# A dense and a dilated attention mixed by a gate, on one core: head pairs in the outer loop instead of query chunks

## The chip, the cores and the metric

The kernel runs on one core of one Trainium2 chip. The time is the device time of one launch in microseconds (us). Of three runs of the kernel before, the median was 818.75 us (816.8 to 819.12). A core has five engines with an instruction queue each: TensorE (PE, matrix products and transposes), VectorE (DVE), ScalarE (ACT), GpSimd (POOL) and SyncE (SP, which issues the transfers here). An engine runs its own instructions in their order and waits on semaphores for the others.

## The reference

Two attentions over the same input, 2048 positions of 512 values, 32 heads of 16. Branch A is dense: every query attends to all 2048 keys. Branch B attends to eight keys at distances 0, 2, ..., 14. A gate per position mixes them.

```python
x = A_x                                     # 1 x 2048 x 512, bf16
g = sigmoid((x * gate_w).sum(-1, keepdims=True))
# A: q, k, v = x @ A_wqkv in 32 heads of 16
scores = einsum("bhqd,bhkd->bhqk", q, k) * 16 ** -0.5
a = softmax(scores) @ v                     # then heads joined, @ A_wo
# B: q, k, v = x @ B_wqkv; idx = pos - (0, 2, ..., 14), masked below 0
logits = einsum("bhsd,bhswd->bhsw", q, k[idx]) * 16 ** -0.5
b = softmax(logits) @ v[idx]                # then heads joined, @ B_wo
return g * a + (1 - g) * b
```

The 32 x 2048 x 2048 exponentials of branch A are the bulk of the work.

## The kernel before

*A planner writes the order.* The program is not written down in loops. Every piece of work is an `Op` (line 73) with an engine, a planned duration, what it depends on, a due time, and the buffers (`Hold`, `Slots`) that it takes and gives back. `Sched.run` (line 253) plays a model of the engines: again and again it takes the engine whose next piece can start soonest, picks among its ready pieces the one due first, and emits it. Each engine's instructions then stand in that order for good: the chip cannot reorder them, it only waits. An `Op` may also have a `not_before` time.

*Branch A* is cut into 32 periods (line 1028): a query chunk `c_` of 512 positions (4 of them, `NC`) and a head group `i` of four heads (8 of them, `NG`). In the old order the chunk is the outer loop and the head group the inner one. In a period, PE makes scores of 128 keys by 512 queries per head (16 key tiles x 4 heads = 64 such units) into PSUM. Most units go to ACT: rings of alternately three and two units (`emit_fill`), one exponential instruction each (tile `pT`). A part goes to DVE instead (`start_quad`, `make_quad`): four units make a quad. DVE computes an exponential by converting to integers that are read as bf16 bit patterns: four conversions (`dt<-m_ps`) and two further terms (`dt<-dt`, shifted). `d_source` starts a quad when DVE has room. PE multiplies all with the values into one accumulator `acc` (`emit_pva`, `emit_pvd`). When a period is through, `post` (line 916) transposes the accumulator on DVE, takes the reciprocal, scales on POOL (`ott`), and, after the second head group of a pair, transposes back into `oat` (128 x 512, bf16): 16 of these, one for each chunk and pair.

*Projections.* Keys of all groups stay in SBUF, in `kt_all` (128 x 8 groups x 2048, bf16), values in `vp_all`. `k_proj` (line 537) makes keys of one group and chunk: 20 matmuls on PE, a cast and a maximum on DVE; `selk` joins the maxima. `v_proj` (line 588) makes values of some heads. `q_proj` (line 633) makes the queries of one period; three buffers. `g_jobs` (line 674) computes the gate. When which is issued is set in `hooks` (line 1393), which is called as a period begins, with due times in units of `TPER` = 23,500 planned ns. In the old order period 0 asks for the keys of all groups, spread over some six periods, and values come in periods 0, 2 and 4; the weights `wo` (`wo_jobs`, line 492) are loaded in period 7 into the place of the weights of keys and values.

*Branch B* comes in 16 tiles of 128 positions (`b_tile`, line 706), beside A. For each, PE projects, DVE copies, SP stores keys and values to a scratch tensor in DRAM, loads them back shifted (`ksh`, `vsh`, eight shifts), and POOL multiplies and adds (`prod`), with small steps on DVE (`smmax`, `smsum`) and ACT (`smexp`) between. POOL's last step makes `obb`; PE transposes it (`fin2`) and DVE copies it to `obt` (128 x 4 x 128). `hooks` starts tile t when 1.7 t <= p + 1.

*Finals.* `final` (line 967) makes 128 rows of the output: PE multiplies `obt` with B's output weights, DVE scales by 1 - g (`fb`), PE multiplies the chunk's four `oat` with `wo`, DVE scales by g and adds (`osb`), SP stores. In the old order it is asked for after each chunk's last head group (`after_post`, line 1430). For the last chunk it is done in two parts: three pairs first, their sums kept in the place of the keys of the first groups (`fa_view`, line 960), and the last pair at the end. `oat` has six buffers and `obt` five.

*Zero passes.* PE's planner adds products with zeros (`zero_pass`, line 1373) where it would otherwise do too little.

Of the kernel before, what the change touches and what calls it, by code (L numbers as in the profile page):

```python
# [20 lines left out]
NG = 8  # L21
W = 8
DIL = 2
QW = 512
# [307 lines left out]
def kernel(  # L332
# [19 lines left out]
    TPC = QW // 128  # L352
    BPC = QW // 32
    WH = W // 2

    const = ctx.enter_context(tc.tile_pool(name="const", bufs=1))
    work = ctx.enter_context(tc.tile_pool(name="work", bufs=2))
# [42 lines left out]

    COL4 = [("c", j, 512) for j in range(4)]
    S_ = Sched()
    for name_, n_ in (("m", 2), ("rA", 1), ("rB", 1), ("acc", 1), ("pTA", 3), ("pTB", 3), ("qt", 3), 
                      ("dt", 8), ("accT", 2), ("ott", 2), ("ksv", 2), ("prod", 1), ("lg", 2),
                      ("kvs", 1), ("qb", 1), ("osb", 3), ("oat", 6), ("obt", 5), ("fb", 1)):
        S_.slots[name_] = Slots(n_)

    def misc_ps(hold, shape, dtype=FP32):
        return ps.tile(shape, dtype, tag=f"m{hold.k}", bufs=1, name=f"m{hold.k}_ps")
# [127 lines left out]
    def k_proj(i, sc, due, first=False):  # L537
        hold = Hold("m")
        st = {}

        def part(c0, c1):
            def s():
                if c0 == 0:
                    st["pk"] = misc_ps(hold, [128, QW])
                    mm_init(st["pk"], e32, QW)
                pk = st["pk"]
                for c in range(c0, c1):
                    for j in range(4):
# [12 lines left out]
        def red():  # L561
            src = st["pk"][:] if first else kt_all[:, i, sc * QW:(sc + 1) * QW]
            V.tensor_reduce(out=kmax_all[:, i, sc:sc + 1], in_=src, axis=AX.X, op=ALU.max, apply_absolute_value=True)
        p1 = Op("PE", part(0, 2), mms=COL4 * 3, deps=xt_ops[sc] + [ld["wk"]], due=due, acq=[hold], name="k1")
        p2 = Op("PE", part(2, DC), mms=COL4 * 2, deps=[p1], due=due, name="k2")
        for o in (p1, p2):
            S_.add(o)
        if first:
            r = S_.add(Op("DVE", red, dur=700.0, deps=[p2], due=due, name="kred"))
            e = S_.add(Op("ACT", evac, dur=650.0, deps=[p2, r], due=due, rel=[hold], name="kev"))  # L570
        else:
            e = S_.add(Op("DVE", evac, dur=690.0, deps=[p2], allow=400.0, rel=[hold], name="kev"))
# [15 lines left out]
    def v_proj(h0, h1, tb, TB, due):  # L588
# [17 lines left out]
            V.tensor_copy(out=vp_all[:, tb:tb + TB, h0:h1, 0:DH], in_=st["pv"][:].rearrange("p t (h d) -> p t h d", d=DH))  # L606
        per = max(1, TB // 2) * DC
        deps = [o for sc in range(tb // TPC, (tb + TB - 1) // TPC + 1) for o in xt_ops[sc]] + [ld["wv"]]
        ops = [Op("PE", mk(0), mms=[("f", None, max(n, 140))] * per, due=due, acq=[hold], name="v1")]
        if TB > 1:  # L610
            ops.append(Op("PE", mk(1), mms=[("f", None, max(n, 140))] * per, due=due, name="v2"))
        ops.append(Op("DVE", evac, dur=690.0, allow=400.0, rel=[hold], name="vev"))
# [85 lines left out]
        g_done.append(ops[-1])  # L698


    kv_store = {}
    obt_tiles, obt_hold, obt_ops = {}, {}, {}
    ob_last = {}
# [2 lines left out]
    def b_tile(t, due):  # L706
# [19 lines left out]
        def store():  # L726
            SP.dma_start(out=kv_scr[16 + t * 128:16 + (t + 1) * 128, :], in_=st["kvs"][:])
        xd = xt_ops[t // TPC] + [ld["bw"]]
        kv = [Op("PE", pj("k", hk, 0, 2), mms=COL4 * 2, deps=xd, due=due, acq=[hk, hkv], name="bk1"),
              Op("PE", pj("k", hk, 2, 4), mms=COL4 * 2, due=due, name="bk2"),  # L730
              Op("DVE", kev, dur=690.0, allow=600.0, rel=[hk], name="bkev")]
        vv = [Op("PE", pj("v", hv, 0, 2), mms=COL4 * 2, deps=xd + [kv[1]], due=due, acq=[hv], name="bv1"),
# [154 lines left out]
                level[-1] += 1  # L887
        padd(fin1, 1264.0, acq=[hobb], rel=[hp[2]])
        hb = Hold("m")
        obt_hold[t] = Hold("obt")  # L890

        def fin2():
            st["ptp"] = misc_ps(hb, [128, DC, 128], BF16)
# [4 lines left out]
                                identity=ident[:], tile_position=(0, 32 * c4))  # L898

        def fin3():  # L900
            obt_tiles[t] = sb(obt_hold[t], [128, DC, 128], BF16, "obt")
            V.tensor_copy(out=obt_tiles[t][:], in_=st["ptp"][:])
        f = [Op("PE", fin2, mms=[("c", j, 128) for _ in range(DC) for j in range(4)], allow=4000.0, acq=[hb, obt_hold[t]], rel=[hobb],
                deps=[pool[-1]], name="bf2"),
             Op("DVE", fin3, dur=420.0, allow=800.0, rel=[hb], name="bf3")]
# [10 lines left out]
    def post(c_, i, pv_ops):  # L916
        acc = acc_tiles[(c_, i)]
        pair, half = (c_, i // 2), i % 2
        hT = Hold("accT")
        st = {}  # L920
        if not half:
            oat_hold[pair] = Hold("oat")
            ott_of[pair] = (Hold("ott"), {})
        ho, so = ott_of[pair]
        last = (c_, i) == (NC - 1, NG - 1)

        def turn():
            accT = sb(hT, [128, BPC, 32], FP32, "accT")
            V.transpose(out=accT[:].rearrange("p b d -> p (b d)"), in_=acc[:])
            st["accT"] = accT  # L930

        def rec():
            rden = work.tile([128, BPC], FP32, name="rden", tag="rden", bufs=3)
            V.reciprocal(out=rden[:], in_=st["accT"][:, :, DH:DH + 1].rearrange("p b o -> p (b o)"))
            st["rden"] = rden

        def scale():
            if not half:
                so["ott"] = sb(ho, [128, BPC, 32], BF16, "ott")
            rd_bc = _ap(st["rden"][:], [list(st["rden"][:].ap[0]), [1, BPC], [0, DH]])  # L940
            (V if last else G).tensor_tensor(out=so["ott"][:, :, half * DH:half * DH + DH], in0=st["accT"][:, :, 0:DH], in1=rd_bc,
                                             op=ALU.mult)

        def back():
            oat_tiles[pair] = sb(oat_hold[pair], [128, QW], BF16, "oat")
            V.transpose(out=oat_tiles[pair][:], in_=so["ott"][:].rearrange("p b d -> p (b d)"))
        a = 0.0 if last else 3000.0
        ops = [Op("DVE", turn, dur=720.0, allow=-2000.0, deps=pv_ops, acq=[hT],
                  rel=[acc_hold[(c_, i)]], name="accT", prompt=True),
               Op("DVE", rec, dur=240.0, allow=a, name="rec"),  # L950
               Op("DVE" if last else "POOL", scale, dur=450.0 if last else 640.0, due=-1.0, acq=[] if half else [ho], rel=[hT],
                  name="scale")]
        if half:
            ops.append(Op("DVE", back, dur=710.0, allow=a, acq=[oat_hold[pair]], rel=[ho], name="oatT"))
        S_.chain(ops)
        if half:
            oat_ops.setdefault(c_, []).append(ops[-1])


    def fa_view(tt):  # L960
        flat = kt_all[:, 0:NG - 1, :].rearrange("p g s -> p (g s)")
        return flat[:, tt * 2 * QW:(tt + 1) * 2 * QW].bitcast(FP32)

    fa_ops = {}
    NPR = NG // 2

    def final(c_, tt, k0, k1, due):

# [56 lines left out]
            fa_ops[tt] = ops[-1]  # L1025


    periods = [(c_, i) for c_ in range(NC) for i in range(NG)]
    NP = len(periods)
    front = [0] * NP  # L1030
    back = [NT] * NP
# [361 lines left out]
    def hooks(p):  # L1393
        now = S_.now
        c_, i = periods[p]
        if p == 0:
            g_jobs(now + 12000.0)
            for g in range(1, NG):
                reds = [k_proj(g, sc, now + TPER * (0.85 * (g - 1) + 0.1 * (sc + 1))) for sc in range(NC)]
                selk(g, reds, now + TPER * (0.85 * (g - 1) + 0.45))  # L1400
        if p == 0:
            q_proj(periods[1][0], periods[1][1], now + 0.4 * TPER)
        if p + 2 < NP:
            q_proj(periods[p + 2][0], periods[p + 2][1], now + 0.6 * TPER)
        if p == 0:
            v_due(4, 8, now, TPER * 0.9)
            v_due(8, 16, now + TPER * 0.3, TPER * 1.5)
        if p == 2:
            v_due(16, 24, now, TPER * 1.8)
        if p == 4:  # L1410
            v_due(24, 32, now, TPER * 1.8)
        if p == NG - 1:
            wo_jobs([o for i_ in range(NG) for o in kt_ops[i_]] + list(vp_ops.values()))
        if p < 31:
            for t in range(NT):
                if 2 * t == p or (p == 0 and t == 0) or (t in (1,) and p == 1):
                    pass
        while b_next[0] < NT and b_next[0] * 1.7 <= p + 1.0:
            b_tile(b_next[0], now + (2000.0 if p > 2 else 12000.0))
            b_next[0] += 1  # L1420

    b_next = [0]

    def v_due(h0, h1, t0, span):
        n = (h1 - h0) * DH
# [3 lines left out]

    def after_post(c_, i):  # L1430
        now = S_.now
        if c_ < NC - 1 and i == NG - 1:
            for tt in range(TPC):
                final(c_, tt, 0, NPR, now + TPER * (0.5 + 0.6 * tt))
        if c_ == NC - 1 and i == NG - 2:
            for tt in range(TPC):
                final(c_, tt, 0, NPR - 1, now + TPER * 0.15 * (tt + 1))
        if c_ == NC - 1 and i == NG - 1:
            for tt in range(TPC):
                final(c_, tt, NPR - 1, NPR, now)  # L1440
# [42 lines left out]
```

## Time and profile before

| | |
|---|---|
| median of three runs | 818.75 us |
| the profiled execution: its time | 817.6 us |
| its span, first to last instruction | 815.5 us |
| mean granted clock of PE | 0.986 |
| busy: PE, DVE, ACT, POOL | 746.9, 677.0, 761.2, 695.1 us |
| first exponential starts | 26.9 us |
| last exponential ends | 802.9 us |
| POOL's first product starts, last ends | 53.8, 804.8 us |

All durations below come from the profiled execution. A row of the groups reads: line, engine, operation, what it writes and reads with the shapes, the count, busy time and mean duration in ns, then the engine's idle time just before these instructions and what ended it. Line 381 is a helper that records each operation, so the groups are told apart by their tiles. A row of the stages reads: from:to, length, busy us and (in brackets) instructions of PE, PE's weight loads, DVE, ACT and POOL, the granted clock, the share of DMA, GB/s. The order of the instructions in both programs can be read from the built programs, without a run; where the text says that something stands "at exponential 32", 32 of ACT's 656 exponential instructions were emitted before it.

### The profile page before, as it was taken

Reading aid. Unit: us, or ns where it says so; the run is one execution under the profiler, and the core shown is the slowest. Engines: PE = TensorE matmul, PEld = TensorE weight load, DVE = VectorE, ACT = ScalarE, POOL = GpSimd, SP = SyncE. Lnnn points to the kernel's source line nnn. Section 1 sums busy time; section 2 is a strip of 40 time slices with the busy share of each in tenths; the row PEclk is TensorE's granted clock in tenths of the full one; section 3 lists DMA queues with packets and bytes.
Section 4 is the critical chain, followed back from the end, with each engine's and each line's share of the span. In section 5 each row is a group of like instructions: output and inputs, shape, how many; then the busy total and the mean of one; then the engine's idle time right before and its main releaser. Section 6 shows DMA issues by size and latency. Waiting matters only on the chain.

```text
span 815.5 us, 20495 instructions
## 1 busy us (share of the span) xinstructions
PE 746.9 (92%) x8593; PEld 242.5 (30%) x8647; DVE 677.0 (83%) x1023; ACT 761.2 (93%) x682; POOL 695.1 (85%) x599
## 2 busy tenths in 40 slices
PE   8899999999989999999999898889998998999896
PEld 3334333333223232222222222222222232222222
DVE  2456677988799887999999897897999889999984
ACT  2798999899799998999999999999999999999993
POOL 1037694986799899999999999999999999999994
PEclk9999999999799999999999999998999999999998
DMA  8020304003211112112122212111211221101100
GB/s 269 18 67 14 105 2 118 2 14 117 79 52 66 47 41 83 41 54 66 52 66 67 65 31 92 37 40 53 66 66 53 59 79 60 52 10 46 52 2 27
DMA packets 44155, 47.47 MB, mean 58 GB/s; under 512 B 2080, under 2 KB 41504, under 8 KB 44064
## 3 DMA queue, kind: packets, MB, share of 16 engines
q1 hardware_dynamic: 44064, 46.18, 17.6%
q8 instruction: 67, 1.10, 0.6%
q14 instruction: 24, 0.20, 0.1%
HBM read 39.85 MB, written 6.32 MB: 57 GB/s over the span
## 4 chain that ended last, share of the span: by engine, by line
ACT 32%; POOL 26%; PE 22%; issue 10%; DVE 9%; POOLq 0%; ACTq 0%; DVEq 0%
ACT pT L381 31%; POOL prod L381 23%; PE m_ps L381 10%; DVE dt L381 7%; PE acc L381 6%; PE ring L381 5%; POOL lg L381 2%; PE warm L381 1%; POOL obb L381 1%; POOL ott L381 1%; PE pxt L381 1%; ACT lg L381 0%; DVE accT L381 0%; DVE osb L381 0%; POOL vp_all L381 0%
## 5 line engine op out<-in xcount | busy, mean ns | idle before, releaser
L381 ACT ACTIVATE pT<-ring 128x1536 bf16<-128x1536 f32 (+1 forms) x656 | 750.7, 1292 | 21.5 <-PE ring L381 19.6
L381 PE MATMUL ring<-qt,kt_all 32*128 32x512 bf16 x1640 | 278.8, 385 | 34.9 <-ACT pT L381 30.2
L381 POOL TENSOR_TENSOR prod<-prod 128x512 f32<-128x512 f32 x224 | 294.0, 1318 | 10.4
L381 DVE TENSOR_SCALAR dt<-m_ps 128x512 uint16<-128x512 f32 x408 | 268.5, 676 | 35.3 <-PE m_ps L381 23.1
L381 POOL TENSOR_TENSOR prod<-ksh,qb 128x512 f32<-128x512 bf16 x128 | 162.7, 1298 | 70.3 <-DMA ksh<-kv_scr 68.2
L381 DVE TENSOR_SCALAR dt<-dt 128x2048 uint16<-128x2048 uint16 x204 | 221.6, 1090 | 0.5 <-PE acc L381 0.3
L381 PEld LDWEIGHTS <-kt_all 32*128 32x128 bf16 x2048 | 86.5, 91 | 281.5 <-issue 274.3
L381 PE MATMUL acc<-pT,vp_all 128*17 128x512 bf16 x1640 | 158.3, 386 | 2.9 <-issue 2.8
L381 POOL TENSOR_TENSOR prod<-vsh,lg 128x512 f32<-128x512 bf16 x128 | 151.7, 1202 | 4.5
L381 PE MATMUL m_ps<-qt,kt_all 32*128 32x512 bf16 x408 | 140.8, 384 | 10.0 <-DVE dt L381 5.8
L381 PEld LDWEIGHTS <-vp_all 128*17 128x17 bf16 x2048 | 46.4, 88 | 107.0 <-issue 97.8
L381 PE MATMUL acc<-dt,vd_all 128*17 128x512 bf16 x816 | 63.2, 385 | 0.1
L381 PE MATMUL m_ps<-bw,xT 128*32 128x512 bf16 x768 | 54.5, 382 | 0.7 <-DVE dt L381 0.7
L381 PE MATMUL acc<-ones_t,zw 128*32 128x512 bf16 (+1 forms) x225 | 47.9, 392 | 2.6 <-issue 1.3
L381 PE MATMUL acc<-dt,vp_all 128*17 128x512 bf16 x408 | 40.7, 389 | 1.0 <-issue 1.0
L381 PEld LDWEIGHTS <-xT 128*32 128x32 bf16 (+1 forms) x1152 | 31.9, 96 | 31.2 <-issue 24.1
L381 PEld LDWEIGHTS <-zw 128*32 128x32 bf16 (+1 forms) x419 | 21.8, 95 | 57.3 <-issue 54.2
L381 PE MATMUL m_ps<-xT,wq 128*16 128x512 bf16 x512 | 38.7, 387 | 0.0
L381 DVE CAST kt_all<-m_ps 128x512 bf16<-128x512 f32 x28 | 19.1, 684 | 22.0 <-PE m_ps L381 21.9
L381 PE MATMUL m_ps<-xT,wkv 128*16 128x512 bf16 x512 | 36.7, 380 | 0.0
L381 DVE CAST qt<-m_ps 128x512 bf16<-128x512 f32 x32 | 21.8, 682 | 10.5 <-PE m_ps L381 10.2
L381 DVE TENSOR_SCALAR absq<-m_ps 128x512 int32<-128x512 int32 x32 | 21.9, 684 | 9.6 <-PE m_ps L381 9.5
(69 smaller groups left out, 476.0 us busy)
## 6 DMA issues: line engine op xcount, KB each, us to landing
ksh<-kv_scr SPq DMA_DIRECT2D x16, 1024.0 KB, 5.5
vsh<-kv_scr SPq DMA_DIRECT2D x16, 1024.0 KB, 5.7
kv_scr<-kvs SPq DMA_DIRECT2D x16, 256.0 KB, 2.0
xld<-in_A_x_dram SPq DMA_DIRECT2D x4, 512.0 KB, 6.5
out_dram<-osb SPq DMA_DIRECT2D x16, 128.0 KB, 1.7
bw<-in_B_wqkv_dram SPq DMA_DIRECT2D x1, 1536.0 KB, 10.2
wkv<-in_A_wqkv_dram SPq DMA_DIRECT2D x2, 512.0 KB, 7.0
wq<-in_A_wqkv_dram SPq DMA_DIRECT2D x1, 512.0 KB, 7.9
```

The costliest lines, as they stand in the source:

```text
L381: return chain_on(key, f(*a, **k))
```

## The change

The periods now run over pairs of head groups outside, chunks inside, and the two groups of a pair innermost. So every pair visits all four chunks, in eight periods, before the next pair starts, and the keys and values of a pair are needed only when its eight periods begin. `hooks` asks for them one pair ahead (new `k_due`, and `v_due`), with a `not_before` so that they can't run much too early. The gate is computed from period 4. The first tile of branch B is due 22 us instead of 12 us after the start, and B's key projections may not start more than 4 us ahead of their due time.

The outputs of all chunks are then finished only with the last pair, so nearly all `oat` and `obt` must be kept. They share one set of places, `keep`: 11 buffers of their own, and 16 places in `kt_all`, in the keys of the first two pairs of groups, which become free when a pair's last chunk is done (`after_post`). The kept sums of the last chunk move to the keys of groups 4 and 5 (`fa_view`). The finals of the first three chunks are asked for when the last pair has finished a chunk, the first part of the last chunk's as chunk 2 is finished. `wo` is loaded as the last pair's eight periods begin.

```diff
+    KEPT = 11
-                      ("kvs", 1), ("qb", 1), ("osb", 3), ("oat", 6), ("obt", 5), ("fb", 1)):
+                      ("kvs", 1), ("qb", 1), ("osb", 3), ("keep", KEPT + 16), ("fb", 1)):
         S_.slots[name_] = Slots(n_)
+    for k in range(KEPT, KEPT + 16):
+        S_.slots["keep"].free[k] = INF
...
-        p1 = Op("PE", part(0, 2), mms=COL4 * 3, deps=xt_ops[sc] + [ld["wk"]], due=due, acq=[hold], name="k1")
+        p1 = Op("PE", part(0, 2), mms=COL4 * 3, deps=xt_ops[sc] + [ld["wk"]], due=due, acq=[hold], not_before=0.0 if first else due - 5000.0,
+                name="k1")
...
+    def kept(hold, name):
+        if hold.k < KEPT:
+            return sb(hold, [128, QW], BF16, name)[:]
+        k = hold.k - KEPT
+        return kt_all[:, k // 4, (k % 4) * QW:(k % 4 + 1) * QW]
...
-        kv = [Op("PE", pj("k", hk, 0, 2), mms=COL4 * 2, deps=xd, due=due, acq=[hk, hkv], name="bk1"),
+        kv = [Op("PE", pj("k", hk, 0, 2), mms=COL4 * 2, deps=xd, due=due, acq=[hk, hkv], not_before=due - 4000.0, name="bk1"),
...
-            oat_tiles[pair] = sb(oat_hold[pair], [128, QW], BF16, "oat")
-            V.transpose(out=oat_tiles[pair][:], in_=so["ott"][:].rearrange("p b d -> p (b d)"))
+            oat_tiles[pair] = kept(oat_hold[pair], "oat")
+            V.transpose(out=oat_tiles[pair], in_=so["ott"][:].rearrange("p b d -> p (b d)"))
...
-        flat = kt_all[:, 0:NG - 1, :].rearrange("p g s -> p (g s)")
+        flat = kt_all[:, 4:6, :].rearrange("p g s -> p (g s)")
...
-    periods = [(c_, i) for c_ in range(NC) for i in range(NG)]
+    periods = [(c_, i) for m in range(NPR) for c_ in range(NC) for i in (2 * m, 2 * m + 1)]
...
         if p == 0:
+            k_due(1, now, 0.35 * TPER)
+            v_due(4, 8, now + 0.5 * TPER, TPER * 0.4)
+            q_proj(periods[1][0], periods[1][1], now + 0.5 * TPER)
+        if p == 4:
             g_jobs(now + 12000.0)
-            for g in range(1, NG):
-                reds = [k_proj(g, sc, now + TPER * (0.85 * (g - 1) + 0.1 * (sc + 1))) for sc in range(NC)]
-                selk(g, reds, now + TPER * (0.85 * (g - 1) + 0.45))
...
+        m = p // 8
+        if p % 8 == 1 and m + 1 < NPR:
+            k_due(2 * m + 2, now + 0.5 * TPER, 4.0 * TPER)
+            v_due(8 * m + 8, 8 * m + 16, now + 1.5 * TPER, 4.5 * TPER)
+            k_due(2 * m + 3, now + 3.0 * TPER, 4.0 * TPER)
...
-        if p == NG - 1:
+        if p == NP - 8:
             wo_jobs([o for i_ in range(NG) for o in kt_ops[i_]] + list(vp_ops.values()))
...
-            b_tile(b_next[0], now + (2000.0 if p > 2 else 12000.0))
+            b_tile(b_next[0], now + (2000.0 if p > 2 else 22000.0))
...
+    def k_due(g, t0, span):
+        reds = [k_proj(g, sc, t0 + span * (sc + 1) / NC) for sc in range(NC)]
+        selk(g, reds, t0 + span + 1000.0)
...
     def after_post(c_, i):
         now = S_.now
+        if i % 2 and i // 2 < 2 and c_ == NC - 1:
+            for k in range(KEPT + 8 * (i // 2), KEPT + 8 * (i // 2) + 8):
+                S_.slots["keep"].give(k, now)
         if c_ < NC - 1 and i == NG - 1:
             for tt in range(TPC):
-                final(c_, tt, 0, NPR, now + TPER * (0.5 + 0.6 * tt))
-        if c_ == NC - 1 and i == NG - 2:
+                final(c_, tt, 0, NPR, now + TPER * (0.2 + 0.4 * tt))
+        if c_ == NC - 2 and i == NG - 1:
             for tt in range(TPC):
-                final(c_, tt, 0, NPR - 1, now + TPER * 0.15 * (tt + 1))
+                final(NC - 1, tt, 0, NPR - 1, now + TPER * (1.0 + 0.2 * tt))
```

`v_proj` has the same kind of `not_before` (5 us) for all heads but the first four; `obt` is placed by `kept` as `oat` is.

More of the change, by code (lines that the diff above doesn't have):

```diff
@@ L354 @@
     WH = W // 2
+    NPR = NG // 2
     const = ctx.enter_context(tc.tile_pool(name="const", bufs=1))
@@ L608, in v_proj @@
         deps = [o for sc in range(tb // TPC, (tb + TB - 1) // TPC + 1) for o in xt_ops[sc]] + [ld["wv"]]
-        ops = [Op("PE", mk(0), mms=[("f", None, max(n, 140))] * per, due=due, acq=[hold], name="v1")]
+        ops = [Op("PE", mk(0), mms=[("f", None, max(n, 140))] * per, due=due, acq=[hold], not_before=due - 5000.0 if h0 else 0.0, name="v1")]
         if TB > 1:
@@ L889, in b_tile @@
         hb = Hold("m")
-        obt_hold[t] = Hold("obt")
+        obt_hold[t] = Hold("keep")
         def fin2():
@@ L900, in fin3 @@
         def fin3():
-            obt_tiles[t] = sb(obt_hold[t], [128, DC, 128], BF16, "obt")
-            V.tensor_copy(out=obt_tiles[t][:], in_=st["ptp"][:])
+            obt_tiles[t] = kept(obt_hold[t], "obt").rearrange("p (c t) -> p c t", c=DC)
+            V.tensor_copy(out=obt_tiles[t], in_=st["ptp"][:])
         f = [Op("PE", fin2, mms=[("c", j, 128) for _ in range(DC) for j in range(4)], allow=4000.0, acq=[hb, obt_hold[t]], rel=[hobb],
@@ L921, in post @@
         if not half:
-            oat_hold[pair] = Hold("oat")
+            oat_hold[pair] = Hold("keep")
             ott_of[pair] = (Hold("ott"), {})
@@ L960, in fa_view @@
     def fa_view(tt):
-        flat = kt_all[:, 0:NG - 1, :].rearrange("p g s -> p (g s)")
+        flat = kt_all[:, 4:6, :].rearrange("p g s -> p (g s)")
         return flat[:, tt * 2 * QW:(tt + 1) * 2 * QW].bitcast(FP32)
     fa_ops = {}
-    NPR = NG // 2
     def final(c_, tt, k0, k1, due):
@@ L1396, in hooks @@
         if p == 0:
+            k_due(1, now, 0.35 * TPER)
+            v_due(4, 8, now + 0.5 * TPER, TPER * 0.4)
+            q_proj(periods[1][0], periods[1][1], now + 0.5 * TPER)
+        if p == 4:
             g_jobs(now + 12000.0)
-            for g in range(1, NG):
-                reds = [k_proj(g, sc, now + TPER * (0.85 * (g - 1) + 0.1 * (sc + 1))) for sc in range(NC)]
-                selk(g, reds, now + TPER * (0.85 * (g - 1) + 0.45))
-        if p == 0:
-            q_proj(periods[1][0], periods[1][1], now + 0.4 * TPER)
+        m = p // 8
[3 more added lines that the diff above has]
+            k_due(2 * m + 3, now + 3.0 * TPER, 4.0 * TPER)
         if p + 2 < NP:
             q_proj(periods[p + 2][0], periods[p + 2][1], now + 0.6 * TPER)
[L1405 to L1411, printed above, removed]
-        if p == NG - 1:
+        if p == NP - 8:
             wo_jobs([o for i_ in range(NG) for o in kt_ops[i_]] + list(vp_ops.values()))
[L1414 to L1417, printed above, removed]
         while b_next[0] < NT and b_next[0] * 1.7 <= p + 1.0:
-            b_tile(b_next[0], now + (2000.0 if p > 2 else 12000.0))
+            b_tile(b_next[0], now + (2000.0 if p > 2 else 22000.0))
             b_next[0] += 1
     b_next = [0]
+    def k_due(g, t0, span):
+        reds = [k_proj(g, sc, t0 + span * (sc + 1) / NC) for sc in range(NC)]
+        selk(g, reds, t0 + span + 1000.0)
     def v_due(h0, h1, t0, span):
```

## The prediction

> **What bounds the kernel now.** I read the page's busy shares first. No engine stands out: ScalarE (ACT) 93%, TensorE (PE) 92%, GpSimd (POOL) 85%, VectorE (DVE) 83%.
>
> ```profile
> PE 746.9 (92%) x8593; PEld 242.5 (30%) x8647; DVE 677.0 (83%) x1023; ACT 761.2 (93%) x682; POOL 695.1 (85%) x599
> ACT 32%; POOL 26%; PE 22%; issue 10%; DVE 9%; POOLq 0%; ACTq 0%; DVEq 0%
> L381 ACT ACTIVATE pT<-ring 128x1536 bf16<-128x1536 f32 (+1 forms) x656 | 750.7, 1292 | 21.5 <-PE ring L381 19.6
> L381 DVE TENSOR_SCALAR dt<-dt 128x2048 uint16<-128x2048 uint16 x204 | 221.6, 1090 | 0.5 <-PE acc L381 0.3
> ```
>
> The second line is the chain that ended last: it passes from engine to engine, so the bound changes along the run. The third says that 656 exponentials of ACT take 750.7 us, 1.144 us each one behind the other (the mean of 1.292 counts overlaps of neighbours twice). ACT is idle for 815.5 - 761.2 = 54.3 us, and that is all that can be won without moving exponentials elsewhere. To place it I cut the run at every 41st exponential (stages by time; columns: from:to, length, then busy us and count of PE, PEld, DVE, ACT, POOL, then clock, DMA share, GB/s).
>
> ```profile
> 26.90:76.60 49.70, 47.48 (x702) 20.14 (x705) 28.71 (x49) 47.06 (x42) 20.63 (x20) 1.00 0.09 28
> 76.60:125.00 48.40, 46.91 (x624) 16.64 (x620) 33.24 (x62) 47.08 (x43) 36.44 (x36) 1.00 0.15 51
> 125.00:177.00 52.00, 49.84 (x641) 17.72 (x635) 43.23 (x70) 47.83 (x43) 40.03 (x38) 1.00 0.16 47
> 177.00:228.60 51.60, 47.58 (x486) 13.79 (x490) 41.78 (x61) 47.24 (x44) 38.07 (x33) 0.90 0.27 83
> ...
> 325.80:708.10 382.30, 349.49 (x3906) 108.00 (x3930) 347.10 (x508) 376.31 (x337) 370.76 (x312) 0.99 0.18 56
> ```
>
> The ACT idle in the first four stages is 2.64 + 1.32 + 4.17 + 4.36 = 12.5 us. In the last line, eight stages long, it is 6.0 us, 0.75 per stage. So ACT is starved early, and it bounds later. Before 26.9 us nothing can be exponentiated, and after the last exponential (802.94 us) the tail takes 12.6 us.
>
> POOL needs its own look, since 85% hides a late start. The timeline has these rows (start, duration; in brackets the idle time before):
>
> ```profile
> 53.83 4.50 POOL L381 TENSOR_TENSOR prod<-ksh,qb 128x512 f32<-128x512 bf16 x4 [50.58 <-DMA ksh<-kv_scr]
> ...
> 803.56 1.26 POOL L381 TENSOR_TENSOR obb<-prod 128x512 bf16<-128x512 f32 x1
> ```
>
> From 53.8 on it works 692 us in a stretch of 751. From 286.3 to 737.3 it starts ten tiles of the branch B, one per 45.1 us, 97% busy. It ends at 804.8, after ACT. It is a second bound.
>
> **The change part by part.** Only the order changes: the built programs have the same counts on ACT (656 exponentials) and DVE (102 quads, that is 408 conversions and 204 terms); PE loses 16 of its zero passes (16 x about 0.2 us, which only keep the clock). So no busy time is saved; I price where the work lands.
>
> *Key and value projections spread.* By exponential 164, 32 key reductions and 16 value copies stand in the old order, 15 and 8 in the new. With the rows 0.684 (cast), 0.678 (reduce) and 0.687 (value copy), 17 x 1.36 + 8 x 0.69 = 28.7 us of DVE move behind that point, and 17 x 20 matmuls of PE. In exchange conversions there rise from 55 to 89 and terms from 25 to 42: 34 x 0.676 + 17 x 1.09 = 41.5 us. DVE was 147 of 202 us busy there (28.7+33.2+43.2+41.8), so it has the room. The PE clutter goes: this row shows what it cost, a new key group's passes ahead of a ring fill at the join of two periods.
>
> ```profile
> 152.22 4.62 ACT L381 ACTIVATE pT<-ring 128x1536 bf16<-128x1536 f32 x4 [3.94 <-PE ring L381]
> ```
>
> Between stages the new order is even: DVE work per stage, from the same rows, is 45 to 51 us from stage 2 to 13, where the old ran from 37 to 52. If the first four stages fall from 12.5 to about 1 us of idle each, as later, ACT gains 8.5 us. The 28.7 us now lie in stages 5 to 12, 3.6 us in each, in the place of the quads that left them; without that cover a key group would cost ACT what it cost at 152 us, up to 4 us.
>
> *Clock.* 5.4 us of the ACT idle lies in two stretches where the granted clock was half: 10.2 us long from 209.6, and 6.8 us from 554.4.
>
> ```profile
> 206.20:209.60 3.40, 2.45 (x16) 0.60 (x14) 3.40 (x5) 3.40 (x4) 3.32 (x3) 1.00 0.69 208
> 209.60:213.00 3.40, 3.40 (x25) 0.66 (x24) 2.00 (x4) 1.85 (x2) 3.16 (x5) 0.51 0.95 229
> ```
>
> A window with 16 matmuls came ahead, another with 20 at 551. The Trainium skill, "TensorE: Matmul & The Clock Gate", Part 1, says that the clock follows PE's activity in windows of 3413 ns, and is either full or half; the stretches here are 3 and 2 such windows. The rule speaks against thinning PE early: the new second stage has 488 matmuls for 640. By the rule alone I would add one more such stretch, +3.6 us. But of the old stages those with 462 to 472 matmuls kept the full clock and those with 483 and 443 lost it, so the sum of a stage doesn't decide; the least filled new stage has 481. I add nothing, and keep -4 to +4 in the range.
>
> *Branch B starts later.* The first tile's projections may not start before 18 us, and are due 10 us later; the first POOL product stands behind exponential 32, before 23 (in the trace it ran behind 24). 9 x 1.21 us (49.7/41) later is 64.7. Nothing covers this but POOL's own waits. Those it had: for the shifted keys 17.6 us after the first wait, for the maxima 10.2, reciprocals 5.4 and 4.6; and new tiles came late up to the sixth. The new order issues the key loads of tiles 2 to 4 at exponentials 77, 117, 138 (before 89, 129, 146), so POOL can be full from its second tile. Two sums: (1) total need: 692 busy / 0.97 = 714, and the first tile's own waits 3.7 + 4.6 + 3.5: 64.7 + 726 = 790. (2) the late pace for all: 64.7 + 35.4 (first tile) + 14 x 45.1 + 67.5 (last start to end, 737.3 to 804.8) = 799. Here a second rule weighs. POOL's products took 1.128 us from 54 to 110, with few terms on DVE, and 1.349 from 330 to 730. The Trainium skill, "SBUF — State Buffer", Who interferes with whom, has DVE's fast forms and GpSimd block each other for a whole instruction. By it every term costs POOL up to the 0.68 us of an undisturbed term. There are 204 in both orders, but fewer fall into POOL's idle time: POOL was idle 18% of the time from 53.8 to 286.3, and so are some 8 of the 44 terms there; now 2 stand ahead of its start, and it has little idle time. 6 x 0.68 = 4 us. The rows alone say 0, the rule 4; I take 3: POOL ends at 793, between 790 and 799.
>
> *Finals.* All 16 output tiles move into the last eight periods (0.74 + 0.75 us of DVE and 32 matmuls each); before, four each followed a chunk. Twelve move, 18 us of DVE, covered by quads moved forward (68 conversions in the last three stages, 89 before). Outputs go into dead keys with the same transpose and copy; in the built program these writes wait for their own producer only, so 0. The eight loads of wo go from exponential 149 to 496 on SP's queue, ahead of the keys of tile 13; these are wanted 5 exponentials (5.9 us) after their issue and land in 5.5: 0 as long as POOL runs 5 to 9 exponentials behind its place, as it did in most of this run, and up to 6 us of POOL if not. The gate's pass moves (0.35 + 1.6 us of ACT idle at 71.8): it stays a loss.
>
> *Tail.* The tail's B passes now overlap: DVE has, from the last accumulator's transpose on, 0.71+0.24+0.52+0.74+0.70+0.75+4 x 0.75 = 6.7 us; before 9.2 (803.55 to 812.78). So 12.6 - 1.9 = 10.7. But the last tile's 16 transposes, which wait for POOL, now stand ahead of the last two ring fills, not behind all: from POOL's end come transposes (0.9), fill (0.5), two exponentials (2.5), tail: 14.6 us, against 10.7 before (804.8 to 815.5).
>
> *Sum.* ACT's way: 802.9 - 8.5 + 10.7 = 805.1. POOL's way: 793 + 14.6 = 807.6. They nearly meet and will disturb each other by a little: I take 808, 7.5 below the span. The execution lasted 817.6, 2.1 more than its span; the median 818.75 is 1.15 above that. 808 + 3.2 = **811**.
>
> **Rivals.**
> - *The idle time only moves.* PE has 92% and DVE 99% of a late stage in the new order; what is won early is lost in small waits at each late key group. For it: ACT waited for the ring 21 times in this run, wherever work met. Against: 0.75 us a stage with 92% DVE. Gain 0 to 2: 818.
> - *POOL's late start decides* (slower). If the 26 us of waits between the second and the last tile are only replaced by others of the same size (today's mean pace there, 648.1/14 = 46.3), POOL ends at 64.7 + 35.4 + 14 x 46.3 + 67.5 = 815.8, and the span at 830: 833. It decides once POOL ends behind 801 (815.5 - 14.6). For it: the maxima of tile 3 now stand 2 exponentials behind the sum that they need, of tile 12 four, where POOL ran 5 to 9 behind its place; DVE would wait there with all that is queued behind it: conversions, projections' evacuations, so ACT. Against: key loads come earlier.
> - *ACT alone bounds*, clock never halved: 805.1 + 3.2 - 4 = 804.
>
> **How the numbers follow.** Forecast 0.52 (own range 806 to 816), idle moves 0.15, POOL decides 0.18 (any size up to 833, mostly under 826), ACT alone 0.15. The range 803 to 826 leaves out the far ends, about 0.2. Within 0.3% is 816.3 to 821.2, about what a measurement here can tell. Faster: 0.50 + 0.15 + 0.03 = 0.68; same: 0.02 + 0.10 + 0.02 = 0.14; slower: 0.02 + 0.16 = 0.18.
>
> **What would show it.** Right: four first stages of 41 exponentials at 47.5 to 49 us; no ring wait of 3 us; first POOL product near 65 and its last near 793, with no gap over 5 us after the second tile; last transposes followed by ring fills, tail near 10.7. Wrong: POOL ending behind 801, DVE waiting for POOL's sums, half-clock stretches in the first 200 us, or ACT idle over 1.5 us a stage behind stage 4.

## The result, and the profile after

The changed kernel takes 807.91 us (median of four runs, 806.77 to 808.3), the kernel before 818.93: ratio 0.986, 95% interval 0.9826 to 0.9894. Run again in another set, it took 809.74 against 818.05: 0.9899, 0.9865 to 0.9933. The forecast was 811, range 803 to 826. The ratios here and below leave out executions over 1.5% above the fastest of their kernel, which stand apart at a lower clock.

The profiled execution's span is 806.3 us, 9.2 less than before. From the page of the changed kernel, the busy shares, the chain, and the same two groups as before:

```profile
PE 752.6 (93%) x8631; PEld 241.0 (30%) x8631; DVE 681.5 (85%) x1023; ACT 760.9 (94%) x682; POOL 695.0 (86%) x599
ACT 35%; PE 29%; DVE 20%; issue 10%; POOL 5%; DMA 0%; ACTq 0%; DVEq 0%; POOLq 0%
L382 ACT ACTIVATE pT<-ring 128x1536 bf16<-128x1536 f32 (+1 forms) x656 | 750.3, 1291 | 17.5 <-PE ring L382 16.0
L382 DVE TENSOR_SCALAR dt<-dt 128x2048 uint16<-128x2048 uint16 x204 | 221.6, 1088 | 1.3 <-PE acc L382 0.6
```

Busy times moved by less than 6 us each; POOL's share of the chain fell from 26% to 5%. The difference is in ACT's idle time. Here are the first four stages of 41 exponentials taken together, the other twelve, and the tail, first of the kernel before, then of the changed one (from:to, length, then busy us of PE, PEld, DVE, ACT, POOL, the clock, DMA share, GB/s):

```profile
26.90:228.60 201.70, 191.81 (x2441) 68.29 (x2450) 146.96 (x239) 189.21 (x170) 135.17 (x125) 0.97 0.17 52
228.60:802.90 574.30, 528.09 (x5849) 162.48 (x5893) 514.82 (x753) 564.36 (x505) 555.33 (x467) 0.99 0.17 53
802.90:815.50 12.60, 5.71 (x67) 2.03 (x65) 7.04 (x11) 0.04 (x1) 1.85 (x2) 0.80 0.12 42
```

```profile
25.60:218.90 193.30, 182.32 (x2140) 61.83 (x2143) 155.10 (x236) 188.14 (x169) 142.71 (x127) 0.98 0.16 52
218.90:795.50 576.60, 545.69 (x6204) 169.12 (x6196) 511.06 (x756) 565.13 (x505) 549.60 (x466) 0.99 0.18 54
795.50:806.30 10.80, 4.19 (x56) 1.35 (x48) 7.16 (x12) 0.00 (x0) 0.00 (x0) 0.74 0.14 49
```

The early part gained 8.4 us, with PE at 2140 matmuls instead of 2441 and DVE at 155 us instead of 147. Of the 8.4 us, 7.3 are ACT's idle time and 1.1 its busy time. The later part lost 2.3, the tail gained 1.8. The remaining 1.3 us is an earlier first exponential (25.6 instead of 26.9). That is no effect of the change: this start came at 25.6, 26.3 and 27.0 us in profiles of the changed kernel and of one with the same start-up, and at 25.7 to 26.9 us in the old order.

Part of the idle time falls into stretches where PE's granted clock was half. Early, these are 209.7 to 219.9 us before (ACT idle for 3.6 of 10.2 us) and 25.9 to 32.8 us after (1.1 of 6.9 us); later, 554.4 to 561.3 us before (1.8 us idle) and 391.2 to 401.4 us after (4.1 us). So at half clock ACT was idle for 5.4 us before and 5.1 after; at full clock the early part fell from 8.9 to 4.1 us and the later from 8.1 to 7.4.

POOL, first and last rows of its work in the timeline of the changed kernel:

```profile
64.80 4.49 POOL L382 TENSOR_TENSOR prod<-ksh,qb 128x512 f32<-128x512 bf16 x4 [4.66 <-DVE dt L382]
...
788.58 1.75 POOL L382 TENSOR_TENSOR obb<-prod 128x512 bf16<-128x512 f32 x1
```

It starts 11 us later than before and ends 14.5 us earlier, at 790.3, before the last exponential and not after it. The last transposes begin at 792.1.

### The profile page after: what moved, and what is told of

Its sections match the earlier page's. It is cut to its first block, busy times and chain, and to the rows that moved or that the text cites. A ratio compares the mean times of both kernels' runs of the same rounds, so it can differ in the third digit from the quotient of the medians.

```text
span 806.3 us, 20526 instructions
## 1 busy us (share of the span) xinstructions
PE 752.6 (93%) x8631; PEld 241.0 (30%) x8631; DVE 681.5 (85%) x1023; ACT 760.9 (94%) x682; POOL 695.0 (86%) x599
## 4 chain that ended last, share of the span: by engine, by line
ACT 35%; PE 29%; DVE 20%; issue 10%; POOL 5%; DMA 0%; ACTq 0%; DVEq 0%; POOLq 0%
ACT pT L382 35%; DVE dt L382 14%; PE m_ps L382 12%; PE acc L382 8%; PE ring L382 7%; POOL prod L382 4%; PE warm L382 1%; DVE kt_all L382 1%; DVE accT L382 1%; DVE qt L382 1%; DVE kvs L382 1%; DVE absq L382 1%; DVE vd_all L382 1%; ACT lg L382 1%; PE pxt L382 0%
## 5 line engine op out<-in xcount | busy, mean ns | idle before, releaser
L382 POOL TENSOR_TENSOR prod<-prod 128x512 f32<-128x512 f32 x224 | 298.0, 1336 | 10.7
L382 PEld LDWEIGHTS <-kt_all 32*128 32x128 bf16 (+1 forms) x2304 | 92.0, 92 | 288.2 <-issue 277.7
L382 POOL TENSOR_TENSOR prod<-ksh,qb 128x512 f32<-128x512 bf16 x128 | 160.4, 1280 | 12.4 <-DVE qb L382 5.3
L382 POOL TENSOR_TENSOR prod<-vsh,lg 128x512 f32<-128x512 bf16 x128 | 151.2, 1197 | 4.7
L382 POOL TENSOR_TENSOR ott<-accT,rden 128x256 bf16<-128x256 f32 x31 | 22.9, 737 | 62.4 <-DVE rden L382 62.3
L382 PE MATMUL acc<-ones_t,zw 128*128 128x512 bf16 (+1 forms) x271 | 62.4, 392 | 3.5 <-DVE accT L382 3.4
L382 PEld LDWEIGHTS <-xT 128*32 128x32 bf16 (+1 forms) x1152 | 34.0, 97 | 28.8 <-issue 21.9
L382 PE MATMUL m_ps<-xT,wkv 128*16 128x512 bf16 x512 | 38.9, 395 | 0.0
L382 PEld LDWEIGHTS <-zw 128*32 128x32 bf16 (+1 forms) x403 | 19.6, 95 | 54.1 <-issue 50.8
L382 DVE CAST kvs<-m_ps 128x512 bf16<-128x512 f32 x32 | 21.8, 681 | 9.4 <-PE m_ps L382 9.3
```

Source lines behind the costliest of these rows:

```text
L382: return chain_on(key, f(*a, **k))
```

## The experiments

Four sets, each beside runs of the kernel before on the same chip. Ratios are to that kernel. "Early idle" is the length of the first four stages less ACT's busy time there: 12.5 us before, 5.2 after. A trace shows one execution of a kernel; a median rests on four or more.

### Order and projections apart

The new order of periods, but the projections asked for as early as before (and without `not_before`):

```diff
-            k_due(1, now, 0.35 * TPER)
-            v_due(4, 8, now + 0.5 * TPER, TPER * 0.4)
+            for g in range(1, NG):
+                reds = [k_proj(g, sc, now + TPER * (0.85 * (g - 1) + 0.1 * (sc + 1))) for sc in range(NC)]
+                selk(g, reds, now + TPER * (0.85 * (g - 1) + 0.45))
...
+            v_due(4, 8, now, TPER * 0.9)
...
-        if p % 8 == 1 and m + 1 < NPR:
```

> The changed kernel with the projections of keys and values asked for as early as in the kernel before, and everything else as changed. It has two quads more (104) and three exponentials fewer (653). If the gain comes from spreading the projections (my theory), the first four stages of 41 exponentials take 199 to 202 us again, as before the change (201.7), where the changed kernel has 193.3; less the 3.4 us of three exponentials, 812 to 816. If it comes from POOL being full from its second tile, or from the new order of the periods as such, it stays at 804 to 808.

Measured: 813.36, 0.9961 (0.9928 to 0.9994).

```profile
26.00:227.90 201.90, 194.25 (x2482) 70.52 (x2481) 152.88 (x248) 188.73 (x169) 144.90 (x133) 0.99 0.17 53
...
181.62 18.43 ACT L382 ACTIVATE pT<-ring 128x1024 bf16<-128x1024 f32 x16 [4.34 <-PE ring L382]
204.11 11.40 ACT L382 ACTIVATE pT<-ring 128x1024 bf16<-128x1024 f32 x10 [4.07 <-PE ring L382]
```

The first line is the stage view, the others rows of ACT's timeline. The early stretch is 201.9 us again, early idle 13.2 (9.9 of it at full clock), as the first theory said. So asking for the projections late wins the early part, and the order of the periods by itself does not. What this kernel still gains over the kernel before, 3.4 us by the medians, is about the three exponentials that it has fewer.

The changed kernel with the first tile of branch B due early again:

```diff
-            b_tile(b_next[0], now + (2000.0 if p > 2 else 22000.0))
+            b_tile(b_next[0], now + (2000.0 if p > 2 else 12000.0))
```

> The changed kernel with the first tile of branch B due 12 us after the start, as before the change. POOL starts near 54 us. One quad fewer, two exponentials more (2.3 us). If ACT sets the end: 807 to 811, though POOL ends some 10 us earlier. If POOL sets it: 798 to 803.

Measured: 810.11, 0.9913 (0.9882 to 0.9944). POOL started at 52.8 us and was through by 771.8, 18.5 us before the changed kernel's, and the time stayed where the repeat of the changed kernel has it (809.74, in another set). This kernel has two exponentials more, so POOL's late start can have cost these 2.3 us, but no more. This rules out that POOL's end alone set the end of the changed kernel.

### How near POOL is

Order kept exactly: the planner is told nothing, and in each half tile one of POOL's additions emits nothing, 32 in all.

```diff
-            padd(ltree(hf, 8, 2, 4), 1255.0, after_last=False)
+            padd(lambda: None, 1255.0, after_last=False)
```

In the changed kernel:

> The changed kernel, the order of all instructions kept, with two of POOL's additions left out in each tile of branch B (32 x 1.33 = 42 us of POOL; part of the sum of products is left out). If ACT sets the end: 804 to 808, POOL ending far ahead of it. If POOL sets it, through its end or through lags in between: under 800.

Measured: 802.09, 0.9839 (0.9774 to 0.9904), below the range of the first theory and above that of the second. POOL's busy time fell by 46 us (695.0 to 649.1), and the medians differ from those of the changed kernel by 6 to 8 us, with intervals that overlap. A part of that is the clock: at a granted clock of 0.992 one execution of this kernel took 802.2 us and one of the changed kernel 806.1.

In the kernel before:

> The kernel before, order kept, with the same two additions left out in each tile of branch B. There POOL ended at 804.8 us, behind the last exponential at 802.9, and B's last passes followed. If ACT's early idle is what the change took away: 814 to 817, since only the tail behind POOL goes. If the kernel before was held by POOL, and the change won by filling POOL: 803 to 809, like the changed kernel.

Measured: 813.59, 0.9953 (0.9917 to 0.9989): 3.2 us, just below the first range and far from the second. It is not the tail that went: in the trace it takes 12.5 us (794.3 to 806.8), for 12.6 before. ACT's two waits for POOL (2.1 us in the kernel before) are gone. The early stretch took 198.3 us here, with an early idle of 9.65 us, 6.9 of it at full clock. So by the medians 3.2 us of the kernel before were POOL's, against the 8 to 11 that the change won: POOL's being full is not the main source of the gain.

The opposite, in the changed kernel:

```diff
                 G.tensor_tensor(out=st["prod"][:, w_, :], in0=st["ksh"][:, hf * WH + w_, :], in1=st["qb"][:], op=ALU.mult)
+                if w_ == 1:
+                    G.tensor_tensor(out=st["prod"][:, w_, :], in0=st["ksh"][:, hf * WH + w_, :], in1=st["qb"][:], op=ALU.mult)
```

> The changed kernel, order kept, with one of POOL's products done twice in each half tile (32 x 1.28 = 41 us more on POOL, the same values). The last transposes waited on nothing by only 1.7 us. If POOL has no more slack than this anywhere, its end moves from 790 to 829 or 831 and the time to 840 to 848. If POOL is well covered by ACT, 808 to 815.

Measured: 841.88, 1.0316 (1.0264 to 1.0368), 32 us over the changed kernel in the same set. The page's chain of this kernel, and two of its ACT waits (us in total, times, longest):

```profile
POOL 66%; PE 12%; ACT 11%; issue 6%; DVE 5%; DMA 0%; POOLq 0%; DVEq 0%; ACTq 0%
...
ACT pT L382 <- PE ring L382: 29.4, 40, 2.0
ACT lg L382 <- POOL lg L382: 14.9, 11, 2.6
```

The 41 us of the expectation were an estimate; POOL's busy time rose by 36.2 us (695.0 to 731.2) and its end moved by 32.7 (790.3 to 823.0). So 36 us more of POOL cost 32 (34 in the span of the profiled executions), while 46 us less won at most 8. ACT and POOL bind together: POOL has 2 to 4 us of slack in the changed kernel, no more. The second wait shows one way: a small exponential of branch B waits for POOL in ACT's queue, and the large ones stand behind it. The mean clock fell to 0.960 in these runs as well. How much of the 32 us comes through it is not separated here.

### What starved ACT early

My theory was PE's clutter: too many projection matmuls ahead of a ring fill (the scores that PE writes for one exponential). Three kernels take it apart in the kernel before, each with the order kept. First, most matmuls of the later key projections are left out:

```diff
                 for c in range(c0, c1):
+                    if i and c < DC - 1:
+                        continue
```

> The kernel before, order kept, with 12 of 16 product matmuls left out in each of the 28 later key projections (336 in all; keys of groups 1 to 7 are then only a part of the sum). All of them stand in the first 123 exponentials; DVE's casts and maxima stay. If PE's clutter starved ACT (my theory), the first three stages fall from 150 to 143 to 146 us and the time by 4 to 7, to 810 to 813. If DVE's casts and maxima of these groups were the cause, or the clock, it stays within 2 us of the kernel before.

Measured: 814.08, 0.9977 (0.9941 to 1.0013). By the medians that is 4.0 us, between the two ranges, and the ratio is not clear of 1. In the profiled execution the first three stages took 151.2 us, where the theory had 143 to 146 and the kernel before 150.1. Then the matmuls stay, and DVE's work on these keys is shortened:

```diff
-                V.tensor_copy(out=o, in_=st["pk"][:])
+                V.tensor_copy(out=o[:, 0:8], in_=st["pk"][:, 0:8])
...
-            src = st["pk"][:] if first else kt_all[:, i, sc * QW:(sc + 1) * QW]
+            src = st["pk"][:] if first else kt_all[:, i, sc * QW:sc * QW + 8]
```

> The kernel before, order and matmuls kept, with the 28 later key casts and maxima of DVE shortened from 512 to 8 columns (most keys of groups 1 to 7 are then zero; POOL zeroes them at the start, where it is idle). That is some 56 x 0.58 = 32 us less of DVE, nearly all of it in the first 123 exponentials. In the run with thinned key matmuls the ring wait near 150 us stayed (3.2 us), behind an accumulator's transpose that stood after two casts in DVE's queue. If DVE's queue is what starves ACT early, the first four stages fall from 201 to 194 to 197 us and the time by 4 to 8 us, to 809 to 814. If neither PE's matmuls nor DVE's casts matter by themselves, it stays within 2 us of the kernel before, and the ring waits near 107 and 150 us stay.

Measured: 813.4, 0.9969 (0.9953 to 0.9986). The time lies in the range for DVE's queue, but it fell by only 3.0 us, and the mean clock was higher (0.993 against 0.989 in this set); the first four stages took 197.7 us, not under 197. And both:

> The kernel before, order kept, with both of the last two: the 336 key matmuls left out, and the 28 key casts and maxima over 8 of 512 columns (keys of groups 1 to 7 are then mostly zero). Each alone gave about 3 us, and the ring wait near 150 us stayed in both (3.2 and 3.4 us, 3.9 before). If the two cover each other there, this one falls under 1.5 us, the first four stages to 195 to 197 us, and the time to 808 to 812. If the wait stays above 2.5 us, it comes from the order itself: the fill stands behind the opening of the next accumulator, whatever lies ahead; then 812 to 815.

Measured: 816.03, 0.9969 (0.993 to 1.0007), 1 us past the second range; the wait stayed, as it said. Rows of ACT's timelines, one from each of the three in this order:

```profile
152.85 15.92 ACT L381 ACTIVATE pT<-ring 128x1536 bf16<-128x1536 f32 x14 [3.17 <-PE ring L381]
```

```profile
152.07 15.98 ACT L381 ACTIVATE pT<-ring 128x1536 bf16<-128x1536 f32 x14 [3.39 <-PE ring L381]
```

```profile
154.32 10.49 ACT L381 ACTIVATE pT<-ring 128x1536 bf16<-128x1536 f32 x9 [3.64 <-PE ring L381]
```

The wait of 3.9 us stays at 3.2 to 3.6 with most of the matmuls gone, most of the casts' work gone, or both. Their load alone is not its cause. In the timeline of the kernel before, the join of the two periods has these rows:

```profile
149.97 1.05 PE L381 MATMUL m_ps<-xT,wkv 128*16 128x512 bf16 x16
150.23 0.70 DVE L381 STREAM_TRANSPOSE accT<-acc 128x512 f32<-128x512 f32 x1
150.98 0.40 PE L381 MATMUL acc<-ones_t,zw 128*32 128x512 bf16 x4
151.53 0.60 PE L381 MATMUL ring<-qt,kt_all 32*128 32x512 bf16 x3
152.22 1.45 ACT L381 ACTIVATE pT<-ring 128x1536 bf16<-128x1536 f32 x1 [3.94 <-PE ring L381]
```

In PE's fixed order, the ring fill stands behind the opening of the next accumulator (its first products, with zeros). The opening needs DVE's transpose of the old accumulator, which needs the last products of a quad, which need DVE's terms. In the kernel before, PE comes to the opening just as the transpose is done: until then it is at work on the keys (first row). So work and chain are about equally long here. With the key matmuls thinned out, PE arrives sooner and waits for the transpose (first row below); with both left out, it waits for a term already at the products before (second row); with the casts alone shortened, PE is at the keys until 151.0 us, as before:

```profile
151.60 0.40 PE L381 MATMUL acc<-ones_t,zw 128*32 128x512 bf16 x4 [0.61 <-DVE accT L381]
```

```profile
151.78 0.39 PE L381 MATMUL acc<-dt,vd_all 128*17 128x512 bf16 x4 [0.75 <-DVE dt L381]
```

Behind the load stands a chain that is nearly as long, and the planner put a fill behind both. The early idle of the three kernels was 9.95, 9.3 and 12.4 us (198.4 - 188.45, 197.7 - 188.38, 201.5 - 189.15), of which 5.1, 6.3 and 7.3 us at full clock. The mean clock was 0.93 in these stages with both left out. In the kernel with less POOL above, which has this same early order with all of its load, the early idle was 9.65 us too (6.9 at full clock). So the lighter load saved little there, 2 us at most against that trace. Nor does the mere number of matmuls decide: the kernel with thinned keys has 2111 of them in the early part, the changed kernel 2140, with 5.2 us of early idle (2.8 in its repeat) instead of 9.95.

So: asking for the projections early goes with orders that leave ACT idle early (12.5, 9.65 and 13.2 us, in both period orders); asking for them late goes with less (5.2, 2.8, 4.9 and 2.2 us in four executions of three kernels). At full clock that is 8.9, 6.9 and 9.9 us against 4.1, 2.8, 2.7 and 2.2. That much is shown. That each microsecond comes from a fill behind an opening is not: I read it at 152 us here and at 204 us in the kernel with early projections. The other wait there, at 181.6, is another piece of order: the gate's 64 matmuls, query and value projections, between two fills, with 3.2 of the 4.3 us at half clock.

### The clock

A repeat of the changed kernel, for comparison in one set:

> The changed kernel again, beside the others of this set: 805 to 810, four first stages of 193 to 195 us. If its lead over the kernel before was one of the day, it comes within 4 us of it.

Measured: 809.74 (ten runs, 806.1 to 815.1), early idle 2.8 us (190.8 - 188.04). More zero passes in it:

```diff
-STREAM = 0.48
-LEAST = 0.42
+STREAM = 0.52
+LEAST = 0.46
```

> The changed kernel with the planner's two thresholds for zero passes raised by 0.04 (34 more matmuls with zeros; one quad more, one exponential fewer, 1.1 us). If half-clock stretches cost 3 to 6 us in most executions, the mean clock rises to 0.993 or more and the time falls to 802 to 805. If they cost nothing to ACT, or zero passes don't prevent them: 806 to 809.

Measured: 807.15 (four runs, 806.6 to 807.4), 0.9877 (0.983 to 0.9924), in the second range; mean clock 0.996 to 0.998. The stages of the other twelve, changed kernel first, from the repeat, then this one:

```profile
217.10:796.60 579.50, 547.78 (x6204) 167.49 (x6196) 511.15 (x754) 565.44 (x505) 549.90 (x468) 0.99 0.17 54
```

```profile
218.50:791.40 572.90, 544.13 (x6186) 168.91 (x6182) 517.03 (x756) 562.93 (x504) 548.85 (x465) 1.00 0.17 54
```

ACT's idle time there is 14.1 us and 10.0; of these, 5.8 and 1.0 us lie at half clock. The last exponential ended 5.2 us earlier than in the repeat (791.4 against 796.6), but the tail took 13.5 us instead of 10.8 in this other order. Of the median 2.6 us went, which the intervals don't separate from nothing. The four executions lie close together, but the next two kernels, with the same thresholds, spread as before.

The same thresholds in the kernel before:

> The kernel before with the thresholds for zero passes raised by 0.04, as in the changed kernel with more zero passes. One quad fewer, two exponentials more (2.3 us). If part of the change's gain was luck with half-clock stretches, this comes near the changed kernel: 809 to 812. If the clock is independent of the change: mean clock 0.992 or more, 813 to 817.

Measured: 815.09 (the seven executions in the ratio), 0.9999 (0.9962 to 1.0035). One of ten executions of this program took 3438 us, with PE's ring matmuls at 1456 ns instead of 385; the profile is of that one, so its stages are not read here. The other nine took 813.9 to 827.2 us at mean clocks from 0.997 down to 0.974, so here the zero passes did not keep the clock. The four at 0.997 took 813.9 to 815.1, in the range for a clock that is independent of the change. The change's gain is thus no luck with the clock: the changed kernel's mean clock (0.988 and 0.984 in its two sets) was no higher than that of the kernel before (0.988), and at 0.990 to 0.991 three executions of it took 806.8 to 807.5 us, nine of the kernel before 815.3 to 816.8.

Last, the raised thresholds in the changed kernel, and the gate's pass in four pieces:

```diff
-        ops = [Op("PE", zmm, mms=[("f", None, 70)] * 64, due=due, deps=[o for v in xt_ops.values() for o in v] + [ld["gw"]],
-                  acq=[hz], name="z"),
+        ops = [Op("PE", lambda q=q: zmm(q), mms=[("f", None, 70)] * 16, due=due + 2000.0 * q,
+                  deps=[] if q else [o for v in xt_ops.values() for o in v] + [ld["gw"]],
+                  acq=[] if q else [hz], name="z") for q in range(4)] + [
```

> The changed kernel with the raised thresholds, and the gate's 64 small matmuls split into four pieces that the planner may spread. In the changed kernel they kept the ring from ACT for 2.2 us near 206 us. If that is so, 803 to 806 (807.2 with the thresholds alone); if another piece of work takes their place, 806 to 808.

Measured: 805.45 (804.7 to 812.2), 0.9878 (0.9835 to 0.992), in the first range. It is the lowest median of the kernels that compute everything, but its interval doesn't part it from the changed kernel or from the one with the thresholds alone, so what the gate's pass cost stays open.

## Why the prediction was right, and where not

- *Early idle.* Forecast: 12.5 us fall to about 4, 8.5 gained. The stages gave 8.4, and the repeat 10.9 (201.7 - 190.8). The place was right. The reason was not: the step said "the PE clutter goes", and priced it as work ahead of a ring fill. The three kernels with this work left out keep the wait. In its place stands an order of the work, with a chain of dependencies at a join of periods as long as the load, that the planner wrote when projections were due early. That the size fits so well is in part luck: 3.6 of the 12.5 us lay at half clock, which the step took off with the rest although the forecast added nothing for the clock; 1.1 us of idle time at half clock came back.
- *Work per stage.* Forecast even, DVE 45 to 51 us by the mean rows. The trace has it lower (155.1 us in the first four, 511.1 in the other twelve, 42.6 each), since means of neighbours that overlap count twice, which the forecast knew for ACT and forgot for DVE. DVE had more room than I gave it.
- *Clock.* Forecast: nothing added. Half-clock stretches took 22.6 us of this execution and 22.2 of that before, counting the tail. They moved (to 26 and 391 us, from 210 and 554) and cost the later stages about what the earlier ones gained from them: the stage from 362.9 to 416.5 took 53.6 us, with 6.5 idle, and is most of why the later part lost 2.3 us. As the forecast had read from the old stages, the number of matmuls in a stage does not decide: stages with 564 and 497 of them lost the clock for a while, one with 492 did not.
- *Branch B.* Start 64.7 forecast, 64.8 measured; end 793 forecast (790 and 799 the two sums), 790.3 measured. The first sum, total need, was right. Of the rule's 4 us for terms that block POOL I had taken 3; POOL's busy time is 695.0 us against 695.1, so the rows, which said 0, were right.
- *Which engine ends.* I took POOL's way, 807.6, as the later one. ACT's way ended it: the last transposes waited for PE's place in its order, 1.8 us behind POOL's end. The earlier start of B (no gain) and less POOL (up to 8) confirm that POOL stands close behind, and the doubled products that 2 to 4 us more is all it takes. ACT's way was forecast as 805.1; with 2.3 us lost to the later stages and 1.3 won at the start it is 806.1.
- *From span to median.* I added 3.2 us to the span, since the kernel before had 2.1 in its execution and a median 1.15 above that. The changed kernel has 1.6. This and the span, 806.3 for 808, make up the 3 us between 811 and 807.9.
- *Finals, kept outputs, wo, tail.* Forecast 0, 0, 0 and 10.7 us. The tail is 10.8, and no wait for a load shows among POOL's. The working of the tail does not add up, though: 9.2 less 6.7 us of DVE is 2.5, and only 1.9 was taken off, with no reason given. The trace has 6.6 us of DVE, but the last accumulator's transpose begins 1.2 us behind the last exponential, not 0.6 as before, and what follows DVE's last step takes 3.0 us instead of 2.7.
- *Signs.* Three stages of the first four took 47.0 to 49.0 us, the fourth 50.1 with the gate's pass in it. No ring wait reached 3 us. Two of the signs of being wrong came all the same: a half-clock stretch in the first 200 us, from 25.9, and more than 1.5 us of ACT idle in two later stages (1.8 in the fifth, 6.5 in the eighth).
- *Rivals.* "The idle time only moves" holds for the half-clock part alone (5.4 us before, 5.1 after). "POOL's late start decides" needed POOL to end behind 801: 36 us of added work brought it there, not the change. "ACT alone bounds", 804, was not reached even with the clock at 0.997 (807.15).

## What to carry to other kernels

When a planner writes the order, undo a change of due times before explaining it by load: the same work, left out with the order kept, may return little (2.6 to 4 us by the medians here, where the change won 8 to 11). A second engine that ends near the first has to be measured from both sides, since taking work from it and adding work to it count differently (at most 8 us for 46 less, 32 for 36 more). And sum an engine's full need from its first possible start; that was closer here (790 for 790.3) than a pace read from one stretch (799).

## What was not expected of the hardware

The time of one program goes with the granted clock of PE from execution to execution. Over the 76 executions of the kernel before in the four sets (812.6 to 827.0 us), time and mean clock have a correlation of -0.89, 5.5 us less for each hundredth of the clock more. Yet ACT is the busiest engine, and its exponentials take 1.45 and 1.02 us inside a half-clock stretch as outside; there they come late, behind the ring fills.

Thirty-four more products with zeros went with a clock of 0.996 to 0.998 in four executions of the changed kernel. The same thresholds in the kernel before left it between 0.974 and 0.997, so they are no sure means. Leaving out 12 of 16 matmuls of 28 projections did not shorten the first three stages (151.2 us against 150.1), and the mean clock was 0.984 against 0.988 in that set. The execution of 3438 us, with matmuls nearly four times as long, has a recorded clock of 1.0; what slowed it stays open.
